# A list schedule with smaller margins in the first batch of an attention and mixture-of-experts kernel

## The chip, the core and the metric

The kernel runs on one core of a Trainium2 chip. The metric is the device time of one execution, in microseconds. The kernel before took 1354.56 us, the median of three runs of 1352.25, 1354.79 and 1354.56 us.

The core has a tensor engine (PE, with PEld for the loading of its stationary operand), a vector engine (DVE), a scalar engine (ACT), GpSimd (POOL) and a queue engine (SP) that issues most of the transfers. Each engine works through its own list of instructions in order; an instruction waits for those of other engines on which it depends.

## The reference

```python
# q, k, v: [8 batches, 8 heads, 576 positions, 64]; tau = 0.02
scores = scale * np.matmul(q, k.transpose(0, 1, 3, 2))
thresh = np.max(scores, axis=-1, keepdims=True) - tau
scores = np.where(scores >= thresh, scores, -1e9)
attn = np.exp(scores - np.max(scores, axis=-1, keepdims=True))
attn = attn / (np.sum(attn, axis=-1, keepdims=True) + 1e-09)
attn_out = np.matmul(attn, v)
# x: the heads of a position side by side, [4608 tokens, 512]
gate = 1.0 / (1.0 + np.exp(-(x @ w_gate)))        # w_gate, w_val: [512, 1536]
return (gate * (x @ w_val) @ w_out)               # w_out: [1536, 512]
```

A softmax whose scores more than tau under the row's maximum are left out, a product with V, and then a gated layer over all tokens. All numbers are fp32.

## The kernel before, in words

**Tiles.** Attention is done in 32 visits, one for each batch and pair of heads. A visit has nine tiles of 128 rows by 576 keys: for each of its two heads a group "00" and "02" (first head), "10" and "12" (second head) of two tiles each, and one leftover tile "l" with the last 64 rows of both heads. For one tile, PE makes the scores into one of two buffers `s` (L591 in batch 0, from plain fp32 operands; L599 from batch 1 on, from operands split in a high and a low part), DVE takes the row maximum (L606), the threshold is made from it (L615, on POOL for the first 36 tiles and on DVE from then on), ACT takes the exponential (L620), and DVE masks and sums in one pass (L623), the last to read `s`. For a group, DVE makes the reciprocals of the sums (L655), POOL scales both tiles (L657), PE transposes them (`tp`, L668; `lk`, L681), ACT copies the transposed tiles out of PSUM (`pt`, `pl`, L630), and after the second head PE multiplies with V (`av`, L704), once for tiles 0 and 1, once for tiles 2, 3 and l. ACT copies this to `xf`, and ACT and POOL split it in a high and a low part, the `x` of the gated layer (L714, L716).

**The gated layer.** Blocks 0, 1 and 2 are batches 0 to 2; a block has 24 units of a product with the gate's or value's weights (`m`, L764) and then its output units (`o`, L807). Batches 3 to 8 (the ninth being the leftover rows) go in pairs (L1006, L1071), with sums of blocks and seven products in place of eight. Batches 0 and 1 hand their x over in SBUF, batch 2 through memory (`xa`), the later ones through memory in another layout; `AWAY` is the first batch that goes through memory.

**Weights.** 36 pieces of weights are converted while attention runs (the helper `convert`): a load, a bit step on POOL (L424), an absolute value on ACT (L428), two bit steps on DVE (L431, L437), the high part on ACT (L449), the low part on POOL (L455; for pieces 18 to 23 on DVE, L451), and a store to memory. Twelve stay in SBUF for block 0. `CONV_IN` gives the due time of piece j of the gate's and value's weights, (first, step).

**What sets the order.** A list scheduler (`Plan`) gets all these operations with an engine, a modelled cost, a key (due time, in tiles) and the buffers that they need. It runs through modelled time: an engine that is free takes, among the operations that are ready and have their buffers, that with the lowest key. An operation is ready when what it depends on is done; if that is on another engine, a margin `LAG` is added for its own engine. The order that comes out is emitted, and nothing is moved after that. A tile's operations have the tile's number as key; the product with V that of the visit's last tile, less 0.7. PE's operations of the gated layer have keys above all of attention, so PE takes one only when none of attention is ready; the layer's other operations go first. `SHIFT` is added to the tile numbers from batch 1 on. `LK` gives the small copy of `lk` to ACT below tile 300 and to DVE above. `AHEAD_TWO` is how many units ahead the weights of the paired blocks are loaded.

Of the kernel before, what the change touches and what calls it, by code (L numbers as in the profile page):

```python
# [43 lines left out]
class Plan:  # L44
# [74 lines left out]
    def run(self):  # L119
        engines = ("PE", "DVE", "ACT", "POOL", "SP")  # L120
        ready = {e: [] for e in engines}
        free = {e: True for e in engines}
        events, now, n, dma = [], 0.0, 0, 0.0
        for o in self.ops:
            if not o.n_deps:
                heapq.heappush(events, (0.0, n, "ready", o))
                n += 1
        self.left = {}
        order = []
        while True:  # L130
            moved = True
            while moved:
                moved = False
                for e in engines:
# [3 lines left out]
                    while ready[e]:  # L138
                        x = heapq.heappop(ready[e])
# [30 lines left out]
            while events and events[0][0] <= now + 1e-9:  # L170
                _, _, kind, x = heapq.heappop(events)
                if kind == "free":
                    free[x] = True
                elif kind == "ready":
                    heapq.heappush(ready[x.eng], (x.key, x.seq, x))
                else:
                    for b in x.bufs:
                        b.users -= 1
                        if not b.users and b.held:
                            self.held[b.tag] -= 1  # L180
                            self.held[b.tag, b.cls] -= 1
                    for s in x.succ:
                        lag = 0.0 if s.eng == x.eng else LAG[s.eng]
                        s.ready = max(s.ready, now + lag + s.lag)
                        s.n_deps -= 1
                        if not s.n_deps:
                            n += 1
                            heapq.heappush(events, (s.ready, n, "ready", s))
# [13 lines left out]
    "w": 8, "t2": 6,  # L202
}
LEAD = 8
CONV_IN, CONV_OUT = (10, 1.5), (56, 3)


EARLY = 16
# [2 lines left out]
PAD = 64  # L211

NPS = 4

AV_COST = 0.0096

# [21 lines left out]

OWN = 12

SHIFT = 50


def LO_DVE(j, out):
# [4 lines left out]

LAG = {"PE": 1.2, "DVE": 0.3, "ACT": 0.08, "POOL": 0.3, "SP": 0.08}  # L250

WARM = 16

FIRST_PAIRS = 4
# [3 lines left out]

SUMS_IN, SUMS_OUT, SUM_KEY = {1: (0,), 2: (1,)}, {0: (0,), 1: (1,)}, 1000

AWAY = 2
AHEAD_TWO = 8

X_BY = ((("POOL",) * 4, ("DVE",)),) + ((("DVE",) * 4, ("DVE",)),) * 2
G_BY = (("POOL", "DVE", "POOL", "DVE"), ("DVE",))
# [19 lines left out]
def kernel(  # L285
# [25 lines left out]
    nc = tc.nc  # L311

    B, NPAIR, P, SK = k.shape
    D = v.shape[-1]
# [70 lines left out]
    op, buf = plan.op, plan.buf  # L385
# [9 lines left out]
    wo_d = {g: dram([P, ND, ND, 2, P], f"wod{g}") for g in range(NFG)}  # L395
    w_sb = {}

    def convert(i, f, key):

# [6 lines left out]
        raw = buf("w", [P, DM, 2], I32, f"wr{name}")  # L406
# [5 lines left out]
        def load():  # L412
# [7 lines left out]
        op("SP", 1.6, key - 6, load, writes=[raw], leave=3)  # L420
        lo, hi = (lambda: raw.ap[:, :, 0]), (lambda: raw.ap[:, :, 1])

        bt = buf("b", [P, DM], F32, f"wb{name}", "conv")
# [5 lines left out]
           reads=[raw], writes=[bt])  # L429
        a = lambda: bt.ap.bitcast(I32)  # L430
# [202 lines left out]
    class Group:  # L633
# [52 lines left out]
        def output(self, c, key):  # L686

            vis, pt, pl = self.vis, self.pt, self.pl
            last = self.tiles[0] != 0
            W = 2 * P + (SL if last else 0)  # L690
            av = buf("b", [P, W], F32, f"av{self.name}", "att")
# [6 lines left out]
                ms += [(2 * P, W, j, lambda h, j=j: c.pt.ap[:, 0, j, sl(h)]) for j in range(NJ)]  # L698
                ms += [(2 * P, W, NJ + 1, lambda h: c.pl.ap[:, 0, sl(h)])]

            def go():
                for i, (a, z, j, m) in enumerate(ms):
                    for h in range(2):
                        nc.tensor.matmul(  # L704
                            av.ap[h * D : (h + 1) * D, a:z], vis.vs.ap[:, j, h], m(h),
                            start=i == 0, stop=i == len(ms) - 1, skip_group_check=True,
                        )

            op("PE", AV_COST * W, key, go,
               reads=[pt, pl] + ([c.pt, c.pl] if last else []) + [vis.vs], writes=[av], also=[vis.xf])  # L710
            last_att[0] = copy(AV(vis.first), W, key, lambda: vis.xf.ap[:, c0 : c0 + W], av, (vis.xf, self.name))

    def split_x(x, c0, c1, xf, key):
# [425 lines left out]

    def conversions():  # L1140
        for j in range(2 * NF):
            convert(j % 2, j // 2, CONV_IN[0] + CONV_IN[1] * j)
        for f in range(NF):
            convert(2, f, CONV_OUT[0] + CONV_OUT[1] * f)

    def attention(vis):
        vis.prepare(LEAD)
# [138 lines left out]
```

## Time and profile before

The profiled execution took 1353.87 us; its span on the core is 1352.1 us and its mean granted TensorE clock 0.992.

| engine | busy, us | share of the span | instructions |
|---|---|---|---|
| PE | 1320.8 | 98% | 8292 |
| PEld | 1084.1 | 80% | 8292 |
| DVE | 954.8 | 71% | 1943 |
| ACT | 726.9 | 54% | 1339 |
| POOL | 630.3 | 47% | 660 |

Transfers moved 317.83 MB. The rows below are read like this. In the windows, each stretch of the span has the busy time of each engine, and in brackets how many instructions began in it; then the granted clock of PE (1.00 is full speed), the share of the time in which the 16 DMA engines were busy, and GB/s. In the groups, an instruction's line, engine and operation stand with what it writes <- what it reads, its shapes and its count; then busy time and the mean duration of one in ns; then the idle time of the engine ahead of it, and what ended most of this. A row of the timeline has the start and the duration in us; in square brackets stands the engine's idle time ahead of it and what ended that. The first 109 us hold batch 0's attention, with the conversions; the first unit of the gated layer starts at 108.72 us, the first output unit of block 0 at 232.7 us.

### The profile page before, as it was taken

To read this page: it belongs to the slowest core of one execution; us is meant where nothing else is said; L and a number is where in the kernel's file an instruction comes from. 1 tells how busy PE (TensorE), PEld (TensorE's weight loads), DVE (VectorE), ACT (ScalarE), POOL (GpSimd) and SP (SyncE) were. 2 spreads that over 40 slices of the span, in tenths; PEclk is the share of its full clock that TensorE was granted. 3 is DMA by queue.
4 is the path that set the end of the run, shared out by engine and by line. 5 is a ranking of instruction groups with operands and counts; after the bars stand their busy time and mean duration, and the time that the engine had idled before them with its cause. 6 is when DMAs were issued, how large, how long until landed. Compare 5 with 4: busy or idle time off the path is not lost.

```text
span 1352.1 us, 23686 instructions
## 1 busy us (share of the span) xinstructions
PE 1320.8 (98%) x8292; PEld 1084.1 (80%) x8292; DVE 954.8 (71%) x1943; ACT 726.9 (54%) x1339; POOL 630.3 (47%) x660
## 2 busy tenths in 40 slices
PE   7879999999999999999999999999999999999998
PEld 4557888888888888888888878888888888888887
DVE  7889868567877777778787763556965569654594
ACT  7878766666766766667776653223532225322242
POOL 6985957956777764967776741101000110001100
PEclk8989999999999999999999999999999999999999
DMA  9879999897978988898897858656695656756564
GB/s 341 279 251 309 311 257 269 233 279 209 264 212 242 261 242 227 250 267 238 238 270 188 241 179 295 205 180 211 201 308 183 201 193 204 249 180 204 186 221 129
DMA packets 140436, 317.83 MB, mean 235 GB/s; under 512 B 22048, under 2 KB 49952, under 8 KB 140320
## 3 DMA queue, kind: packets, MB, share of 16 engines
q1 hardware_dynamic: 140176, 316.33, 76.5%
q8 instruction: 67, 1.10, 0.4%
q14 instruction: 49, 0.40, 0.1%
q10 hardware_dynamic: 144, 0.00, 0.0%
HBM read 210.37 MB, written 54.53 MB: 196 GB/s over the span
## 4 chain that ended last, share of the span: by engine, by line
PE 87%; DMA 6%; DVE 2%; ACT 2%; issue 1%; POOL 1%; SPq 1%; ACTq 0%; DVEq 0%; POOLq 0%
PE m L764 13%; PE qb L1006 11%; PE av L704 11%; PE s L599 8%; PE qc L1006 7%; PE qa L1006 7%; PE tp L668 7%; PE o L807 6%; PE rb L1071 5%; PE rc L1071 4%; PE ra L1071 4%; DMA wo<-wod 2%; DMA kd<-k 2%; PE s_l L599 1%; PE lk L681 1%
## 5 line engine op out<-in xcount | busy, mean ns | idle before, releaser
L657 POOL TENSOR_SCALAR p<-p,zero_t,sm 128x576 f32<-128x576 f32 x256 | 216.3, 856 | 107.9 <-DVE sm L655 76.5
L606 DVE TENSOR_REDUCE st<-s 128x1 f32<-128x576 f32 x256 | 192.3, 754 | 91.9 <-PE s L599 83.2
L623 DVE SCALAR_TENSOR_TENSOR p<-s,st,p 128x576 f32<-128x576 f32 x256 | 205.9, 812 | 30.2 <-ACT p L620 23.9
L620 ACT ACTIVATE p<-s,st 128x576 f32<-128x576 f32 x256 | 190.2, 750 | 57.4 <-DVE st L606 56.5
L919 POOL TENSOR_TENSOR gA<-gA 128x512 f32<-128x512 f32 x18 | 24.1, 1341 | 416.2 <-DVE gA L985 416.2
L630 ACT COPY pt<-tp 128x512 f32<-128x512 f32 x256 | 147.4, 589 | 54.0 <-PE tp L668 51.9
L599 PE MATMUL s<-kd,qd 128*128 128x288 f32 x896 | 165.0, 308 | 3.7 <-issue 1.6
L668 PE MATMUL tp<-ident,p 128*128 128x128 f32 x1024 | 156.7, 282 | 2.5 <-POOL p L657 2.0
L764 PE MATMUL m<-x,wi 128*128 128x512 f32 x576 | 158.9, 403 | 0.0
L668 PEld LDWEIGHTS tp<-ident,p 128*128 128x128 f32 x1024 | 123.2, 143 | 29.4 <-POOL p L657 7.6
L599 PEld LDWEIGHTS s<-kd,qd 128*128 128x128 f32 x896 | 133.9, 190 | 14.6 <-DVE p_l L623 2.4
L704 PE MATMUL av<-pt,vs 128*64 128x256 f32 x1024 | 126.1, 389 | 0.0
L807 PE MATMUL o<-g,wo 128*128 128x512 f32 x432 | 117.5, 401 | 0.0
L943 DVE TENSOR_TENSOR qu<-qb,qp 128x512 f32<-128x512 f32 x72 | 49.8, 692 | 89.9 <-PE qb L1006 77.1
L764 PEld LDWEIGHTS m<-x,wi 128*128 128x128 f32 x576 | 99.9, 189 | 14.3
L1006 PE MATMUL qa<-xs_p,wa 128*128 128x512 f32 x432 | 109.6, 389 | 0.0
L704 PEld LDWEIGHTS av<-pt,vs 128*64 128x64 f32 x1024 | 68.6, 138 | 48.5 <-issue 7.5
L1006 PEld LDWEIGHTS qa<-xs_p,wa 128*128 128x128 f32 x432 | 81.1, 188 | 16.8
L807 PEld LDWEIGHTS o<-g,wo 128*128 128x128 f32 x432 | 75.5, 189 | 10.9
L630 ACT COPY xf<-av 128x256 f32<-128x256 f32 x64 | 25.6, 399 | 77.4 <-PE av L704 73.1
L911 ACT CAST gs_p<-gA 128x512 fp32r<-128x512 f32 x54 | 32.4, 620 | 64.5 <-DVE gA L985 26.5
L981 ACT ACTIVATE gA<-qa 128x512 f32<-128x512 f32 x18 | 10.8, 598 | 103.4 <-PE qa L1006 103.4
(148 smaller groups left out, 2628.3 us busy)
## 6 DMA issues: line engine op xcount, KB each, us to landing
kd<-k SPq DMA_DIRECT2D x112, 320.0 KB, 6.0
wi<-wid SPq DMA_DIRECT2D x48, 512.0 KB, 6.9
wo<-wod SPq DMA_DIRECT2D x36, 512.0 KB, 7.0
wa<-wid SPq DMA_DIRECT2D x36, 512.0 KB, 4.1
ws<-sid SPq DMA_DIRECT2D x36, 512.0 KB, 4.5
wt<-sid SPq DMA_DIRECT2D x36, 512.0 KB, 3.3
wo_p<-sod SPq DMA_DIRECT2D x36, 512.0 KB, 4.6
qd<-q SPq DMA_DIRECT2D x112, 128.0 KB, 4.6
```

The costliest lines, as they stand in the source:

```text
L599: nc.tensor.matmul(s.ap[:, c, :HALF], st(), mv(slice(kc + c * HALF, kc + (c + 1) * HALF)), start=m == 0, stop=m == len(steps) - 1,)
L606: op("DVE", 0.76, key, lambda: nc.vector.tensor_reduce(out=st.ap[:, 0:1], in_=sv(), axis=AX.XY, op=ALU.max, negate=True), reads=[s], write ...
L620: op("ACT", 0.74, key, lambda: nc.scalar.activation(p(), sv(), AF.Exp, bias=st.ap[:, 0:1], scale=1.0), reads=[s, (st, 0)], writes=[(g.p, i)])
L623: op("DVE", 0.9, key, lambda: nc.vector.scalar_tensor_tensor(out=p(), in0=sv(), scalar=st.ap[:, 1:2], in1=p(), op0=ALU.is_ge, op1=ALU.mult ...
L630: return op("ACT", act(n), key, lambda: nc.scalar.copy(dst(), src.ap), reads=[src], writes=[part])
L657: op("POOL", 0.9, key, lambda i=i: nc.gpsimd.tensor_scalar(out=p.ap[:, i * S : (i + 1) * S], in0=p.ap[:, i * S : (i + 1) * S], scalar1=zer ...
L668: nc.tensor.matmul(tp.ap[:, c, :], self.p.ap[:, o + c * P : o + (c + 1) * P], ident, is_transpose=True, start=c == 0, stop=c == NJ - 1, sk ...
L704: nc.tensor.matmul(av.ap[h * D : (h + 1) * D, a:z], vis.vs.ap[:, j, h], m(h), start=i == 0, stop=i == len(ms) - 1, skip_group_check=True,)
L764: nc.tensor.matmul(m.ap, wv[:, a, c * P : (c + 1) * P], xs[c].ap[:, z, c0:c1], start=e == 0, stop=e == 11,)
L807: nc.tensor.matmul(acc.ap, wv[:, f, a], g[fg * ND + f].ap[:, z], start=(fg, f, a, z) == (0, 0, 0, 0), stop=(fg, f, a, z) == (NFG - 1, ND - ...
L1006: nc.tensor.matmul(acc.ap, wv[:, y, (2 * h + c) * P : (2 * h + c + 1) * P], xt[prod][c].get()[:, z], start=e == 0 and prod in FIRST, stop= ...
L1071: nc.tensor.matmul(acc.ap, w.ap[:, e, c, y], gt[prod][2 * g + c].get()[:, z], start=m == 0 and g == 0 and prod in FIRST, stop=m == 5 and g ...
```

## The change

Six edits of numbers and one of code:

- A margin of its own, `FRONT_LAG`, holds for an operation whose key is under 36, which is batch 0: 0.3 for PE in place of 1.2, 0.2 for DVE and POOL in place of 0.3. The others keep `LAG`.
- In batch 0 the product with V is handed to the scheduler in three parts of about equal count, with a key later by 1.5 and a modelled cost by columns.
- `CONV_IN` goes from (10, 1.5) to (12, 2.6): piece j is due 2 + 1.1 j tiles later.
- `SHIFT` goes from 50 to 15: batch 1's tiles and all later ones have numbers lower by 35. The last visits thereby fall under tile 300, and 20 small copies go from DVE to ACT.
- `AWAY` goes from 2 to 1: batch 1 too hands its x over through memory.
- `AHEAD_TWO` goes from 8 to 7.
- An operation that depends on none starts at its own `lag`; this is 0 for all, and so are `NOT_YET` and `OUT_NOT_YET`.

```diff
-                heapq.heappush(events, (0.0, n, "ready", o))
+                heapq.heappush(events, (o.lag, n, "ready", o))
...
-                        lag = 0.0 if s.eng == x.eng else LAG[s.eng]
+                        lag = 0.0 if s.eng == x.eng else (FRONT_LAG if s.key < FRONT else LAG)[s.eng]
...
-CONV_IN, CONV_OUT = (10, 1.5), (56, 3)
+CONV_IN, CONV_OUT = (12, 2.6), (56, 3)
...
+AV_PARTED, AV_PARTS, AV_LATE = 1, 3, 1.5
...
-SHIFT = 50
+SHIFT = 15
...
 LAG = {"PE": 1.2, "DVE": 0.3, "ACT": 0.08, "POOL": 0.3, "SP": 0.08}
 
+FRONT, FRONT_LAG = 36, {"PE": 0.3, "DVE": 0.2, "ACT": 0.08, "POOL": 0.2, "SP": 0.08}
+
+NOT_YET, OUT_NOT_YET = (0.0, 0.0), 0.0
...
-AWAY = 2
-AHEAD_TWO = 8
+AWAY = 1
+AHEAD_TWO = 7
...
-            def go():
-                for i, (a, z, j, m) in enumerate(ms):
-                    for h in range(2):
-                        nc.tensor.matmul(
-                            av.ap[h * D : (h + 1) * D, a:z], vis.vs.ap[:, j, h], m(h),
-                            start=i == 0, stop=i == len(ms) - 1, skip_group_check=True,
-                        )
-
-            op("PE", AV_COST * W, key, go,
-               reads=[pt, pl] + ([c.pt, c.pl] if last else []) + [vis.vs], writes=[av], also=[vis.xf])
+            n = AV_PARTS if vis.b < AV_PARTED else 1
+            step = -(-len(ms) // n)
+            for lo in range(0, len(ms), step):
+                def go(lo=lo):
+                    for i in range(lo, min(lo + step, len(ms))):
+                        a, z, j, m = ms[i]
+                        for h in range(2):
+                            nc.tensor.matmul(
+                                av.ap[h * D : (h + 1) * D, a:z], vis.vs.ap[:, j, h], m(h),
+                                start=i == 0, stop=i == len(ms) - 1, skip_group_check=True,
+                            )
+
+                cost = AV_COST * W if n == 1 else 0.2 + 0.0018 * sum(z - a for a, z, *_ in ms[lo : lo + step])
+                op("PE", cost, key + (AV_LATE if n > 1 else 0), go,
+                   reads=[pt, pl] + ([c.pt, c.pl] if last else []) + [vis.vs], writes=[av], also=[vis.xf])
```

Three places show how the order moves. In the names the first number behind the letter is the pair of heads, then the group, in it the tile, and last a running number; the lines of the changed kernel lie 6 to 12 higher from L591 on.

**First piece: PE at the end of batch 0**, from the last product with V (`av_3_12`) to the first unit of the gated layer (`m_0_0_0`); `s_0`, `tp_0` and `lk_0` are batch 1's already. Before:

```order
L704 MATMUL av_3_12_1362<-pt_3_02_1212,vs_3_559 64x256 x8
L704 MATMUL av_3_12_1362<-pl_3_02_1233,vs_3_559 64x128 x4
L704 MATMUL av_3_12_1362<-pt_3_l_1170,vs_3_559 64x64 x8
L704 MATMUL av_3_12_1362<-pl_3_l_1173,vs_3_559 64x64 x2
L668 MATMUL tp_0_000_1403<-ident,p_0_00_1289 128x128 x4
L668 MATMUL tp_0_001_1412<-ident,p_0_00_1289 128x128 x4
L681 MATMUL lk_0_00_1420<-ident,p_0_00_1289 128x128
L599 MATMUL s_0_021_1425<-kd_0_0_686,qd_0_0_950 128x288 x4
L764 MATMUL m_0_0_0_1457<-x_0_572,ws_0_320 128x512 x3
L764 MATMUL m_0_0_0_1457<-x_1_873,ws_0_320 128x512 x3
```

Now:

```order
L715 MATMUL av_3_12_1367<-pl_3_02_1237,vs_3_548 64x128 x4
L715 MATMUL av_3_12_1367<-pt_3_l_1173,vs_3_548 64x64 x8
L715 MATMUL av_3_12_1367<-pl_3_l_1177,vs_3_548 64x64 x2
L605 MATMUL s_0_020_1414<-kd_0_0_677,qd_0_0_955 128x288 x4
L605 MATMUL s_0_021_1424<-kd_0_0_677,qd_0_0_955 128x288 x4
L674 MATMUL tp_0_000_1434<-ident,p_0_00_1307 128x128 x4
L674 MATMUL tp_0_001_1445<-ident,p_0_00_1307 128x128 x4
L687 MATMUL lk_0_00_1455<-ident,p_0_00_1307 128x128
L674 MATMUL tp_0_l_1462<-ident,p_0_l_1379 128x128 x4
L687 MATMUL lk_0_l_1471<-ident,p_0_l_1379 128x128
L605 MATMUL s_0_100_1479<-kd_0_1_969,qd_0_1_1137 128x288 x4
L776 MATMUL m_0_0_0_1487<-x_0_557,ws_0_324 128x512 x3
```

The product still stands as one run. Ahead of the first unit there are now the transposes of `0_l` and the scores of tile `0_100`, which stood behind eight of the unit's matmuls.

**Second piece: ACT in the first visit**, from the exponential of tile `0_00` on. Before:

```order
L620 ACTIVATE p_0_00_215<-s_0_001_204,st_0_001_213 128x576
L558 ACTIVATE qp_1_186<-qp_1_186,scale_t 128x576 x2
L620 ACTIVATE p_0_l_245<-s_0_l_228,st_0_l_239 128x576
L620 ACTIVATE p_0_02_248<-s_0_020_235,st_0_020_243 128x576
L428 ACTIVATE wb_0_257<-wr_0_192 128x512
L630 COPY pt_0_00_263<-tp_0_000_251 128x4x128
L630 COPY pt_0_00_263<-tp_0_001_265 128x4x128
L630 COPY pl_0_00_280<-lk_0_00_271 128x128
L620 ACTIVATE p_0_02_248<-s_0_021_276,st_0_021_290 128x576
```

Now:

```order
L626 ACTIVATE p_0_00_215<-s_0_001_203,st_0_001_213 128x576
L626 ACTIVATE p_0_l_247<-s_0_l_230,st_0_l_242 128x576
L564 ACTIVATE qp_1_190<-qp_1_190,scale_t 128x576
L636 COPY pt_0_00_257<-tp_0_000_250 128x4x128
L636 COPY pt_0_00_257<-tp_0_001_259 128x4x128
L636 COPY pl_0_00_274<-lk_0_00_267 128x128
L564 ACTIVATE qp_1_190<-qp_1_190,scale_t 128x576
L626 ACTIVATE p_0_02_280<-s_0_020_238,st_0_020_245 128x576
L434 ACTIVATE wb_0_291<-wr_0_199 128x512
```

The exponential of tile `020` (the first of `p_0_02`) stood ahead of the copies of `pt_0_00`; now it stands behind them, the copy of `pl_0_00` and the second scaling of `qp_1`.

**Third piece: POOL at the end of batch 0**, from the thresholds of the last tiles to the low part of the last `x` (`x_3`). Before:

```order
L615 TENSOR_SCALAR st_3_121_1237<-st_3_121_1237,ntau_t 128x1
L424 TENSOR_SCALAR wa_0_1259<-wr_0_1210,zero_t 128x512
L455 TENSOR_TENSOR ws_1_1269<-wa_1_1103,ws_1_1269 128x512
L657 TENSOR_SCALAR p_3_12_1235<-p_3_12_1235,zero_t,sm_3_12_1243 128x576 x2
L424 TENSOR_SCALAR wa_1_1315<-wr_1_1219,zero_t 128x512
L657 TENSOR_SCALAR p_0_00_1289<-p_0_00_1289,zero_t,sm_0_00_1311 128x576 x2
L424 TENSOR_SCALAR wa_0_1387<-wr_0_1313,zero_t 128x512
L518 TENSOR_TENSOR k_1_1357<-kn_1_450,k_1_1357 128x640
L716 TENSOR_TENSOR x_3_1417<-xf_3_1325,x_3_1417 128x512
```

Now:

```order
L621 TENSOR_SCALAR st_3_121_1250<-st_3_121_1250,ntau_t 128x1
L430 TENSOR_SCALAR wa_1_1279<-wr_1_1229,zero_t 128x512
L663 TENSOR_SCALAR p_3_12_1252<-p_3_12_1252,zero_t,sm_3_12_1277 128x576 x2
L461 TENSOR_TENSOR ws_1_1291<-wa_1_1179,ws_1_1291 128x512
L430 TENSOR_SCALAR wa_2_1335<-wr_2_1267,zero_t 128x512
L524 TENSOR_TENSOR k_1_1359<-kn_1_516,k_1_1359 128x640
L430 TENSOR_SCALAR wa_0_1383<-wr_0_1319,zero_t 128x512
L663 TENSOR_SCALAR p_0_00_1307<-p_0_00_1307,zero_t,sm_0_00_1317 128x576 x2
L663 TENSOR_SCALAR p_0_l_1379<-p_0_l_1379,zero_t,sm_0_l_1409 128x576
L728 TENSOR_TENSOR x_3_1422<-xf_3_1333,x_3_1422 128x512
```

The low part of a weight (`ws_1`) stood ahead of the scaling of `p_3_12` and now stands behind it. The keys `k_1` stand ahead of the scaling of `p_0_00` in place of behind it, and the scaling of `p_0_l` stands ahead of `x_3`.

More of the change, by code (lines that the diff above doesn't have):

```diff
@@ L396, with convert @@
     w_sb = {}
-    def convert(i, f, key):
+    def convert(i, f, key, not_yet=0.0):
         name = f"{f}_{i}"
@@ L418, in load @@
                 )
-        op("SP", 1.6, key - 6, load, writes=[raw], leave=3)
+        op("SP", 1.6, key - 6, load, writes=[raw], leave=3, lag=not_yet)
         lo, hi = (lambda: raw.ap[:, :, 0]), (lambda: raw.ap[:, :, 1])
@@ L1141, in conversions @@
         for j in range(2 * NF):
-            convert(j % 2, j // 2, CONV_IN[0] + CONV_IN[1] * j)
+            convert(j % 2, j // 2, CONV_IN[0] + CONV_IN[1] * j, max(0.0, NOT_YET[0] + NOT_YET[1] * j))
         for f in range(NF):
-            convert(2, f, CONV_OUT[0] + CONV_OUT[1] * f)
+            convert(2, f, CONV_OUT[0] + CONV_OUT[1] * f, OUT_NOT_YET)
     def attention(vis):
```

## The prediction

> **What bounds the kernel now.** I read the page first, then the span cut into windows.
>
> ```profile
> span 1352.1 us, 23686 instructions
> PE 1320.8 (98%) x8292; PEld 1084.1 (80%) x8292; DVE 954.8 (71%) x1943; ACT 726.9 (54%) x1339; POOL 630.3 (47%) x660
> ```
>
> ```profile
> core 0: us, PE busy (x) PEld busy (x) DVE busy (x) ACT busy (x) POOL busy (x), PEclk, DMA share, GB/s
> 0.00:10.00 10.00, 6.48 (x34) 4.88 (x34) 3.41 (x10) 4.63 (x7) 1.24 (x8) 1.00 0.79 254
> 10.00:20.00 10.00, 7.91 (x43) 4.96 (x43) 8.96 (x20) 9.06 (x17) 8.31 (x13) 0.83 1.03 411
> 20.00:30.00 10.00, 7.33 (x34) 4.30 (x34) 9.83 (x18) 8.14 (x16) 10.00 (x14) 0.69 1.02 373
> 30.00:40.00 10.00, 9.84 (x98) 6.24 (x94) 8.68 (x18) 8.72 (x17) 8.93 (x13) 0.97 0.88 303
> 40.00:50.00 10.00, 6.98 (x36) 4.41 (x37) 8.50 (x19) 7.90 (x16) 9.59 (x15) 0.83 0.74 256
> 50.00:60.00 10.00, 7.41 (x64) 4.70 (x64) 9.42 (x21) 7.85 (x16) 7.79 (x12) 1.00 0.93 285
> 60.00:70.00 10.00, 8.52 (x79) 5.28 (x75) 8.90 (x20) 8.19 (x17) 9.30 (x13) 1.00 0.87 297
> 70.00:80.00 10.00, 8.80 (x74) 5.48 (x76) 9.87 (x21) 8.36 (x16) 9.29 (x14) 1.00 0.90 248
> 80.00:90.00 10.00, 7.42 (x69) 4.77 (x66) 8.31 (x18) 7.41 (x15) 8.82 (x13) 0.93 0.94 292
> 90.00:100.00 10.00, 7.50 (x41) 5.93 (x41) 7.68 (x18) 7.37 (x15) 7.44 (x11) 0.73 0.44 176
> 100.00:110.00 10.00, 9.68 (x96) 7.76 (x93) 9.82 (x22) 8.63 (x19) 7.79 (x8) 1.00 0.79 265
> 110.00:230.00 120.00, 118.06 (x786) 97.96 (x785) 97.25 (x215) 85.25 (x160) 81.30 (x80) 1.00 0.97 292
> 230.00:300.00 70.00, 70.00 (x543) 58.49 (x542) 45.81 (x115) 44.81 (x86) 53.69 (x56) 1.00 0.93 250
> 300.00:700.00 400.00, 398.64 (x3101) 334.21 (x3100) 304.56 (x721) 274.89 (x521) 279.55 (x288) 1.00 0.85 242
> 700.00:817.00 117.00, 115.46 (x882) 95.50 (x880) 81.20 (x207) 70.59 (x124) 73.06 (x74) 1.00 0.73 214
> 817.00:1347.00 530.00, 530.00 (x2343) 438.98 (x2339) 331.93 (x494) 165.10 (x284) 54.23 (x40) 1.00 0.64 211
> ```
>
> From 817 to 1347 us PE is busy all of 530.00. Over 110 to 817 it idles 1.94 + 0 + 1.36 + 1.54 = 4.8 us. In the first 110 us its column adds up to 87.9: 22.1 us idle. PE's work is the same in both kernels, and behind 110 us there is always some of it ready, so the end moves by what the idle time of the first 110 us moves, and by any new idle time later. DVE is the fullest engine there: from 10 to 110 us its column is 90.0, so 10.0 us of it are free. The waits of PE up to 105 us say what it mostly stood for (total, times, longest):
>
> ```profile
> PE s L591 <- DVE p L623: 13.0, 12, 2.4
> ```
>
> Scores have two buffers; one comes free when the masking pass (L623) on DVE has read it. PE waits for DVE, DVE for PE and ACT: a ring.
>
> **The change part by part.** Shares of DVE up to 104 us, by groups:
>
> ```profile
> L623 DVE SCALAR_TENSOR_TENSOR p<-s,st,p 128x576 f32<-128x576 f32 x34 | 27.3, 814 | 4.9 <-ACT p L620 2.3 <-POOL st L615 2.0 <-POOL ws L455 0.4
> L606 DVE TENSOR_REDUCE st<-s 128x1 f32<-128x576 f32 x34 | 25.0, 752 | 5.5 <-PE s L591 4.7 <-PE s L599 0.7
> L431 DVE SCALAR_TENSOR_TENSOR wb<-wb,wa 128x512 int32<-128x512 int32 x19 | 13.1, 689 | 0.4 <-ACT wb L428 0.2
> ```
>
> *Less work in the front? No.* The new due times for weights (12 + 2.6j) look as if conversions left the first batch. By the order they don't: before the last mask of batch 0, DVE has 36 reductions, 36 masks and 18 pairs of conversion steps before, 19 after. A pair is two steps of one shape, 2 x 0.69 = 1.4 us more. So nothing but DVE's 10.0 us can be gained, the 19th pair coming off the stretch behind.
>
> *The three parts of the product: 0.* All eight products of batch 0 stand as one run of 12 or 22 matmuls in the new order too (the first piece of order above shows the last): no score got between the parts. Parting removes no instruction; the late key (+1.5) is spent by the smaller margin, and the products stand one tile of scores earlier. If a part did wait for an own signal, it would cost a few tenths each; I take 0.
>
> *First visit: a loss.* ACT at the start of before:
>
> ```profile
> 12.06 0.73 ACT L620 ACTIVATE p<-s,st 128x576 f32<-128x576 f32 x1
> 13.24 1.07 ACT L630 COPY pt<-tp 128x512 f32<-128x512 f32 x2
> 14.19 0.29 ACT L630 COPY pl<-lk 128x128 f32<-128x128 f32 x1
> ```
>
> ```profile
> 11.07 1.97 PE L668 MATMUL tp<-ident,p 128*128 128x128 f32 x8
> ```
>
> Now the exponential that began at 12.06 stands behind two copies, a small copy and a second scaling (second piece of order). The copies need the transposes, which end at 11.07 + 1.97 = 13.04. So 13.04 + 0.54 (second copy, half of 1.07) + 0.29 + 0.7 (the scaling, of the exponential's shape, by its 0.73) gives 14.6: 2.5 us late. Its mask, the score buffer behind the mask and the next conversion step are queued behind it. Going on by hand through the new order with these durations, I find the ninth tile 2.5 us late.
>
> *Visits 2 to 4: regained.* One of DVE's longest waits further on in before:
>
> ```profile
> 86.49 0.82 DVE L623 SCALAR_TENSOR_TENSOR p<-s,st,p 128x576 f32<-128x576 f32 x1 [1.00 <-ACT p L620]
> ```
>
> In the new order one or two conversion steps (0.69 each) stand between the reductions and the masks at such places, so DVE has work while ACT makes the exponential. By hand the lag falls to about 1.2 us at tile 27 and 0.7 at the last mask of batch 0, with the 19th pair done: 0.7 us ahead in work.
>
> *The tail of batch 0: a gain.* Rows of before:
>
> ```profile
> 96.05 0.81 DVE L623 SCALAR_TENSOR_TENSOR p<-s,st,p 128x576 f32<-128x576 f32 x1
> 97.78 1.28 POOL L455 TENSOR_TENSOR ws<-wa,ws 128x512 fp32r<-128x512 f32 x1 [2.07 <-DVE st L606]
> 99.04 1.65 POOL L657 TENSOR_SCALAR p<-p,zero_t,sm 128x576 f32<-128x576 f32 x2
> 106.94 0.80 DVE L623 SCALAR_TENSOR_TENSOR p_l<-s_l,st_l,p_l 128x576 f32<-128x576 f32 x1
> 107.80 1.27 POOL L716 TENSOR_TENSOR x<-xf,x 128x512 fp32r<-128x512 f32 x1
> 108.72 2.11 PE L764 MATMUL m<-x,ws 128*128 128x512 f32 x8
> 112.33 0.77 PE L599 MATMUL s<-kd,qd 128*128 128x288 f32 x4
> ```
>
> The last mask ends at 96.86, but its scaling on POOL starts at 99.04, behind a conversion (97.78) that was itself waiting. In the new order that conversion stands behind the scaling (third piece of order): with the mask at 97.5, scaling starts at 97.7, 1.3 us sooner. But POOL now has the scaling of the leftover tile ahead of x's low part, and that waits for its mask, which by hand through DVE's order ends at 106.4 (107.7 in before). The scaling (0.8) ends at 107.4, and x's low part at 107.4 + 1.27 = 108.7, against 109.07: of the 1.3 us, 0.4 are left for x. The score of tile 100 needs the mask of tile 020, by hand at 108.6, so that the first m starts at about 109.7. PE meanwhile does tp_l, lk_l and one more score, which in before came behind the first eight m. Eight m, these and that score are done at 112.33 + 0.77 = 113.1 in before, and by hand at 109.7 + 2.11 = 111.8 now: **1.3 us sooner**.
>
> *The rest: 0, with room.* Batch 1's x now goes through memory too, 4 stores and 4 loads like these:
>
> ```profile
> xa<-xa SPq DMA_DIRECT2D x4, 256.0 KB, 6.7
> ```
>
> 2.1 MB at 292 GB/s is 7 us of transfers where the DMA share is already 0.97; block 1's first unit comes only 30 tiles after block 0's first output unit, which covers it; uncovered, one landing, 6.7 us, would show. The earlier batch 1 (SHIFT) puts more tiles between the units of block 0: 49 tiles over its 24 input units for 37 before; PE has work in either mix. AHEAD_TWO 7 still loads several units ahead, where PE is busy 530.00 of 530. The zero allowances move nothing. Twenty small copies go from DVE to ACT in the last batch, both far from full there.
>
> **Sum.** 1353.87 (the profiled execution, 1.77 over its span; the median shown, 1354.56, is 0.7 above it) - 1.3 = **1352.6 us**. Bounds: if nothing of the first visit's 2.5 us comes back and the tail gives 1.3, +1.2, so 1355.1; if all of DVE's 10.0 us goes, 1343.9.
>
> **Rivals.**
>
> *A, the ring closes.* Window 70 to 80 has DVE at 9.87 of 10 with pairs of scores, the pattern that the new order has from tile 20 on. If 10 us free become 3, less 1.4 for the 19th pair: -5.6, so 1348.3. Against it: the first visit starts late, and half of the front is like 70 to 80 already. Chance 0.24.
>
> *B, the clock.* The granted clock is 0.83, 0.69, 0.97, 0.83, 0.93 and 0.73 in six of the windows; busy time by the missing share is 1.3 + 2.3 + 0.3 + 1.2 + 0.5 + 2.0 = 7.6 us of PE. If the long waits vanish, half of it goes with them: 1352.6 - 3.8 = 1348.8. Against: DVE, not PE, is the fullest. Chance 0.14. The Trainium skill (TensorE: Matmul & The Clock Gate, part 1) has the clock halved only after an idle window of about 3.4 us. Here the longest single wait was 2.4 us and the clock fell all the same, so the trace doesn't bear that limit out; by it this rival would be worth nothing.
>
> *C, slower: the wait moves behind the front.* Groups from 110 to 230 us of before:
>
> ```profile
> L599 PE MATMUL s<-kd,qd 128*128 128x288 f32 x128 | 23.2, 304 | 0.8 <-DVE p L623 0.6 <-DVE p_l L623 0.2
> L668 PE MATMUL tp<-ident,p 128*128 128x128 f32 x120 | 18.1, 275 | 0.0
> L704 PE MATMUL av<-pt,vs 128*64 128x256 f32 x96 | 11.7, 385 | 0.0
> L615 DVE TENSOR_SCALAR st<-st,ntau_t 128x1 f32<-128x1 f32 x33 | 6.9, 210 | 0.6
> ```
>
> A tile costs PE 23.2/32 + 18.1/30 + 11.7/32 = 1.7 us and DVE 0.81 + 0.75 + 0.21 = 1.8. Twelve more tiles between the units of block 0 make the window of 120 us 140 long and DVE's 97.25 some 118.5: from 81% to 84.5%. At 81% PE idled 1.6% (1.94 of 120); at 90%, from 10 to 110 us, 18.6%. On the line between, 84.5% costs 8.2% of 140 us: 11.5, and 9.5 more than now. The margins there are unchanged, so I take two thirds: 1352.6 + 6.3 = 1358.9. It decides once PE idles over 4 us between block 0's first input and first output unit. Chance 0.16.
>
> **Numbers.** The forecast has 0.46, mostly 1350 to 1357. A change under 0.2% (2.7 us about the median: 1351.9 to 1357.3) can't be told from none. A and B, with the forecast's lower edge (0.03): faster 0.41. C with the upper edge: slower 0.15. The rest, 0.44: same. The range, 1346.5 to 1358.5, leaves out half of A's lower side and the upper half of C.
>
> **What would show it.** Right: first m at 109 to 110 us with a tp_l and one score more ahead of it; a mask about 2 us later near 13 us; PE's wait for DVE masks still 10 us or more; products in single runs. Wrong: first m before 106 (A), PEclk near 1.00 in all windows to 110 (B), or more than 4 us of PE idle between 110 and 260 (C).

## The result: slower, and the profile after

The changed kernel took 1362.97 us, the median of four runs from 1361.77 to 1364.24. The kernel before, with one run more beside it, has 1354.67 us. The ratio is 1.0055, with an interval of 1.0033 to 1.0078. The forecast was 1352.6 with a range of 1346.5 to 1358.5: wrong in sign, and outside the range. The time of rival C (1358.9) is the nearest.

The page of the profile of the changed kernel, an execution of 1364.24 us:

```profile
span 1362.5 us, 23701 instructions
PE 1325.5 (97%) x8292; PEld 1085.2 (80%) x8292; DVE 954.0 (70%) x1923; ACT 733.6 (54%) x1359; POOL 626.9 (46%) x660
```

PE does the same 8292 matmuls. The span is 10.4 us longer: PE's busy time is 4.7 us longer and its idle time 5.7. Part of the former is the clock: by its record PE had 27.3 us at half clock ahead of 1340 us, in place of 20.5, which is worth up to 3.4 us; the rest of it was not traced. The windows of the changed kernel say where; of the columns, the busy times of PE, PEld, DVE, ACT and POOL come first:

```profile
0.00:110.00 110.00, 86.19 (x630) 56.44 (x630) 90.33 (x186) 86.88 (x161) 87.61 (x125) 0.89 0.85 289
110.00:230.00 120.00, 115.50 (x816) 94.35 (x816) 100.08 (x216) 83.98 (x159) 72.86 (x74) 1.00 0.92 276
230.00:300.00 70.00, 70.00 (x524) 59.34 (x519) 52.70 (x128) 49.18 (x93) 57.51 (x59) 1.00 0.87 267
300.00:700.00 400.00, 395.31 (x3003) 329.42 (x3001) 290.28 (x689) 264.57 (x503) 274.34 (x283) 1.00 0.83 243
700.00:817.00 117.00, 117.00 (x893) 98.54 (x892) 86.61 (x208) 79.33 (x152) 77.25 (x80) 1.00 0.72 212
817.00:1347.00 530.00, 530.00 (x2390) 437.88 (x2389) 331.91 (x498) 169.71 (x294) 57.31 (x43) 1.00 0.64 213
```

Up to 110 us PE idles 23.8 us, against 22.1 before. From 110 to 817 it idles 4.5 + 0 + 4.7 + 0 = 9.2 us, against 4.8. The larger part of the new idle time, 4.4 of 5.7 us, stands where the prediction had put nothing. PE's waits in the changed kernel (total, times, longest), up to 112 us and then from 112 to 830:

```profile
PE s L597 <- DVE p L629: 7.9, 11, 2.1
PE tp L674 <- POOL p L663: 4.4, 6, 1.1
PE tp_l L674 <- POOL p_l L663: 2.5, 3, 1.3
```

```profile
PE tp L674 <- POOL p L663: 3.0, 3, 1.6
PE s L605 <- DVE p_l L629: 1.3, 1, 1.3
PE tp_l L674 <- ACT xf L636: 1.3, 1, 1.3
```

In batch 0, 5 us of waiting for the mask are gone, and waiting for POOL's scaling came in their place (6.9 us, 1.8 before). Behind it, PE stops for single waits of 1 to 1.6 us. One of them, from POOL's and PE's timelines of the changed kernel:

```profile
409.23 1.29 POOL L800 TENSOR_TENSOR g<-th,g 128x512 fp32r<-128x512 f32 x1
415.01 1.28 POOL L870 TENSOR_TENSOR s<-wi 128x512 f32<-128x512 f32 x1 [4.48 <-DMA wi<-wid]
416.26 1.63 POOL L663 TENSOR_SCALAR p<-p,zero_t,sm 128x576 f32<-128x576 f32 x2
...
417.15 0.66 PE L674 MATMUL tp<-ident,p 128*128 128x128 f32 x4 [1.64 <-POOL p L663]
```

POOL stands 4.48 us at `s`, a sum of two parts of a weight that the paired blocks need only hundreds of microseconds later. The weight has not landed. The scaling of `p`, which attention needs now, stands behind it in POOL's list, and PE waits for that. The plan lets a sum start only behind its load, but it has loads land sooner than they do: the scheduler gives a load of 512 KB 1.5 us to start, 1.7 on one common channel and 0.9 to land, while the page of before has 6.9 us from issue to landing for `wi`.

### The profile page after: what moved, and what is told of

It is laid out like the page before. It is cut to its first block, busy times and chain, and to the rows that moved or that the text cites. A ratio compares the mean times of both kernels' runs of the same rounds, so it can differ in the third digit from the quotient of the medians.

```text
span 1362.5 us, 23701 instructions
## 1 busy us (share of the span) xinstructions
PE 1325.5 (97%) x8292; PEld 1085.2 (80%) x8292; DVE 954.0 (70%) x1923; ACT 733.6 (54%) x1359; POOL 626.9 (46%) x660
## 4 chain that ended last, share of the span: by engine, by line
PE 84%; DMA 4%; POOL 3%; DVE 3%; issue 2%; ACT 2%; SPq 1%; POOLq 0%; ACTq 0%; DVEq 0%
PE m L776 12%; PE qb L1018 11%; PE av L715 9%; PE s L605 7%; PE qc L1018 7%; PE qa L1018 7%; PE tp L674 7%; PE o L819 6%; PE rb L1083 5%; PE rc L1083 4%; PE ra L1083 4%; DMA wr<-in_moe_w_out_dram 2%; PE s_l L605 1%; POOL p L663 1%; PE lk L687 1%
## 5 line engine op out<-in xcount | busy, mean ns | idle before, releaser
L612 DVE TENSOR_REDUCE st<-s 128x1 f32<-128x576 f32 x256 | 192.8, 754 | 93.3 <-PE s L605 83.8
L931 POOL TENSOR_TENSOR gA<-gA 128x512 f32<-128x512 f32 x18 | 24.1, 1340 | 409.3 <-DVE gA L997 409.3
```

Source lines behind the costliest of these rows:

```text
L612: op("DVE", 0.76, key, lambda: nc.vector.tensor_reduce(out=st.ap[:, 0:1], in_=sv(), axis=AX.XY, op=ALU.max, negate=True), reads=[s], write ...
```

## Experiments

Ratios are to the kernel before, run on the same chip beside each group. "Sums waiting" is how long POOL stood for a load ahead of a sum `s<-wi`, from 112 to 830 us. The first sum of any weight starts at 227 us or later in every trace.

### Which part of the change

The change without its part behind batch 0 (margins and the three parts stay):

```diff
-CONV_IN, CONV_OUT = (12, 2.6), (56, 3)
+CONV_IN, CONV_OUT = (10, 1.5), (56, 3)
-SHIFT = 15
+SHIFT = 50
-AWAY = 1
-AHEAD_TWO = 7
+AWAY = 2
+AHEAD_TWO = 8
```

> Only the margins below key 36 and the three parts are changed; due times of weights, SHIFT, AWAY and AHEAD_TWO as before. Theory F (the loss is made in batch 0 and by the margins alone): about 1363 us, as the changed kernel. Theory M (two losses: some 4 us in the first 115 us from the margins, and some 6 us behind it, because batch 1 goes through memory and its attention runs ahead of the gated layer): first unit 3 to 4 us later than 108.7 and PE idle from 110 to 230 us as before (about 2 us), so 1358 to 1359. Theory O (each edit only reshuffles the order, and single stalls decide): anything from 1353 to 1363, with the loss at another place.

Measured: 1.0070 (1.0048 to 1.0091). The other way round, with the margins and the product of before:

```diff
-AV_PARTED, AV_PARTS, AV_LATE = 1, 3, 1.5
+AV_PARTED, AV_PARTS, AV_LATE = 0, 3, 1.5
-FRONT, FRONT_LAG = 36, {"PE": 0.3, "DVE": 0.2, "ACT": 0.08, "POOL": 0.2, "SP": 0.08}
+FRONT, FRONT_LAG = -9, {"PE": 0.3, "DVE": 0.2, "ACT": 0.08, "POOL": 0.2, "SP": 0.08}
```

> Margins and product with V as before; CONV_IN, SHIFT, AWAY and AHEAD_TWO as in the change. Theory F: about 1354.7, as before. Theory M: the first 110 us cost at most 1 us more than before, PE idles 4 us or more between 110 and 230, and the time is 1359 to 1360. Theory O: no fixed place; 1353 to 1363.

Measured: 1.0067 (1.0044 to 1.0091). Either half alone costs as much as the whole; both medians (1365.94 and 1366.55 us) lie above the 1363 that theory O allowed, beside 1356.64 for before. Then the memory path: taken out of the change, and put alone into the kernel before.

```diff
-AWAY = 1
+AWAY = 2
```

> The changed kernel, but batch 1 hands its x over in SBUF again (AWAY 2). In the order the units of block 0 then end at tile 79 in place of 91 (78 in the kernel before). Theory F: no change, 1363. Theory M: the 6 us behind the front go away and the 4 us of the front stay: 1357 to 1358, with PE idle from 110 to 230 near 2 us. Theory O: 1353 to 1363.

> The kernel before, with batch 1 handed over through memory (AWAY 1) and nothing else. In the order the first 190 rows of PE are those of before; block 0's first output unit stands at tile 83 in place of 78. Theory F: 1354.7. Theory M: front as before to 0.3 us, and part of the 6 us behind it, since fewer tiles come in between than with SHIFT 15: 1356 to 1359. Theory O: 1353 to 1363.

Measured: 1.0052 (1.0033 to 1.0071) without it, and 1.0037 (1.0019 to 1.0056) for it alone. In the fourth run the first 190 rows of PE are those of before, the first unit starts at 108.7 us as before, and the time is lost all the same. The last part, the smaller margins without the three parts and without the rest:

> The kernel before with the smaller margins alone (product with V in one part). Theory M: the front loses 3 to 4 us up to 115 us, as in the run with margins and parts together (2.4). Parts as the cause: the front is as before to 1 us. Behind the front, Theory O: 4 us or more are lost in addition, 1360 to 1366; Theory M: nothing more, 1358.

Measured: 1.0042 (1.0024 to 1.0061), the first unit at 116.5 us, and 35.9 us of sums waiting. No part has a price of its own that adds to the others. Theories F and M fall: F since the rear alone loses, M since taking a part out gives nothing back.

### Edits without purpose

If every edit loses, the edit may not matter. Two, and later a third, that change a number of the kernel before by 1 to 3%:

```diff
-LAG = {"PE": 1.2, "DVE": 0.3, "ACT": 0.08, "POOL": 0.3, "SP": 0.08}
+LAG = {"PE": 1.22, "DVE": 0.3, "ACT": 0.08, "POOL": 0.3, "SP": 0.08}
```

> The kernel before with PE's margin 1.22 in place of 1.2: an edit with no purpose. The order of PE differs from row 39 on. Theory O (the order of before is an uncommonly good draw; an edit of any kind gives a new draw, which is usually worse by 4 to 10 us through waits of over 1 us behind the front): 1357 to 1365, and PE idle from 110 to 830 us of 6 us or more in place of 4.9. Theory M (margins and memory each have their own price): 1353 to 1357, as before.

```diff
-AV_COST = 0.0096
+AV_COST = 0.0097
```

> The kernel before with the modelled cost of the product with V at 0.0097 a column in place of 0.0096: also without purpose. Theory O: 1357 to 1365, with waits at other places than in the run with the margin 1.22. Theory M: 1353 to 1357.

```diff
-LAG = {"PE": 1.2, "DVE": 0.3, "ACT": 0.08, "POOL": 0.3, "SP": 0.08}
+LAG = {"PE": 1.2, "DVE": 0.3, "ACT": 0.08, "POOL": 0.31, "SP": 0.08}
```

> The kernel before with POOL's margin 0.31 in place of 0.3: a third edit without purpose. Theory O: 1357 to 1365, and sums waiting for loads over 18 us. Theory M (before is no special draw): 1353 to 1357.

Measured: 1.0050 (1.0033 to 1.0067), 1.0016 (0.9999 to 1.0034), 1.0059 (1.0036 to 1.0082). Two of the three lose as much as the change. The order of before is a better draw than these neighbours, and the reading that fits all these runs is that the change is slower because it left this order; the second of the three edits can't be told from before. In the run with POOL's margin 0.31 a wait for a load reaches PE most plainly, with the weights of the output units (POOL and PE, timelines of that run):

```profile
591.86 1.26 POOL L858 TENSOR_TENSOR s_o<-wo 128x512 f32<-128x512 f32 x1 [7.01 <-DMA wo<-wod]
593.11 1.63 POOL L657 TENSOR_SCALAR p<-p,zero_t,sm 128x576 f32<-128x576 f32 x2
...
593.99 0.48 PE L668 MATMUL tp<-ident,p 128*128 128x128 f32 x1 [3.65 <-POOL p L657]
```

A sum stands 7.01 us for its load, the scaling stands behind it, and PE is idle for 3.65 us.

### More margin for PE

The other reading was that PE's margin of 1.2 us is too small for a plan that is off by several. Doubled behind batch 0, in the kernel before:

```diff
-LAG = {"PE": 1.2, "DVE": 0.3, "ACT": 0.08, "POOL": 0.3, "SP": 0.08}
+LAG = {"PE": 2.4, "DVE": 0.3, "ACT": 0.08, "POOL": 0.3, "SP": 0.08}
...
+FRONT, FRONT_LAG = 36, {"PE": 1.2, "DVE": 0.3, "ACT": 0.08, "POOL": 0.3, "SP": 0.08}
```

> The kernel before with PE's margin doubled to 2.4 from batch 1 on; batch 0 keeps 1.2 and its first 130 rows on PE. Theory W (behind the front PE stops where the plan is off by more than its margin): the waits between 130 and 700 us fall below 2 us, no clock window at half there, 1353 to 1356 unless the filler runs out at the end of attention (16 matmuls of output units are left behind it in place of 72). Theory O: just another draw, 1357 to 1365.

Measured: 1.0026 (1.0007 to 1.0046). The trace was of an execution with a span of 1352.4 us, and PE's idle time from 110 to 830 us was only 2.0. A second trace was taken without any edit, and one each of the kernel before and of the change:

> The order with PE's margin 2.4 behind the front once more. Its first trace had a span of 1352.4 us, with 2.0 us of PE idle from 110 to 830 us and 2.7 us behind, while its timed runs had a median of 1360. Theory C: the second trace is nearer to 1358 in span, with more windows at half clock in the first 115 us. Theory W alone: 1353 again.

> The kernel before once more, for a second trace of one and the same order. Theory C (executions of one order differ because the clock is granted in fixed windows of 3.4 us, whose phase against the kernel is chance): the order of waits is the same, but other windows up to 115 us are at half clock, and the span differs from 1352.1 by what these windows hold of PE, up to 4 us. If the waits themselves differ (transfers), idle time of PE moves by as much instead.

> The changed kernel once more, timed in the same way as the experiments. 1.004 to 1.008 of before. Theory O and C: the first 115 us again 2 to 4 us behind before, the waits behind the front at mostly the same places (near 165 and 575 us), and other windows at half clock.

Measured: the wide margin's second span is 1362.7 us, with 9.1 us idle from 110 to 830. So the low first value was one execution and not the order, and theory W, which gave 1353 to 1356, falls: the timed runs have a median of 1359.97. The change in its second timing has 1.0038 (1.0020 to 1.0057), its span there 1357.8. And the kernel before, the same order instruction by instruction, now shows:

```profile
span 1360.0 us, 23686 instructions
```

That is 7.9 us more than the trace from which the prediction was made. Single runs of the kernel before in the five groups of experiments lie between 1350.4 and 1364.97 us, with medians from 1355.2 to 1357.4. Of these 135 runs 20 were under the first trace's 1353.87 us, and 5 over the second's 1361.84: a low one and a high one of the same kernel. In the second trace ACT stood for a load, and PE behind it:

```profile
624.61 0.72 ACT L514 CAST k<-kn 128x640 fp32r<-128x640 f32 x1 [4.39 <-DMA kd<-k]
...
627.49 0.73 PE L764 MATMUL m<-x,wi 128*128 128x512 f32 x2 [1.28 <-ACT xf L630]
```

Theory C (only the phase of the clock's windows makes the difference) is not enough: PE had 20.5 us at half clock in both traces of before, and in that stretch the waits themselves moved, and by a load.

### The sums later

The test of theory D, that POOL stands at sums whose weights have not landed: the two first sums of a weight become ready in the plan 4 us later than their load's modelled landing, and nothing else is edited. First in the kernel before, then in the change:

```diff
-        def add(cost, out, x, y, sign, reads, writes):
+        def add(cost, out, x, y, sign, reads, writes, lag=0.0):
...
-            ), reads=reads, writes=writes)
+            ), reads=reads, writes=writes, lag=lag)
...
-            add(1.3, lambda t=t: full(t, 0), lambda x=x: full(x, 0), lambda x=x: full(x, 1), 1, [x], [t])
+            add(1.3, lambda t=t: full(t, 0), lambda x=x: full(x, 0), lambda x=x: full(x, 1), 1, [x], [t], 4.0)
```

> The kernel before, with 4 us of margin for the sums of weights on POOL behind the load that they read (0.3 before). The order is the same up to row 367 of PE. Theory D (behind the front POOL stands at a sum whose weights have not landed, 12.3 us in all in the trace of before, with the scaling of p queued behind it, and PE waits for that): POOL's waits of sums for loads fall under 5 us from 112 to 830 us, PE's waits for POOL there go to under 0.5 us, and the time is 1352 to 1356, not slower than before. Theory O (just another draw): 1357 to 1364.

> The changed kernel with the same 4 us of margin for the sums. Its traces have 19.8 and 27.4 us of POOL's sums waiting for loads and 2 to 4 us of PE waiting for POOL behind the front. Theory D: these go under 8 and under 0.5 us, and 3 to 4 us of the 6 come back, 1357 to 1359. Theory O: 1357 to 1366, whatever the waits.

Measured: 0.9989 (0.9968 to 1.0011) and 0.9978 (0.9963 to 0.9994). The change with this one margin is no longer slower than the kernel before; its median is 1355.57 us, beside 1357.42, and lower than the 1357 to 1359 that theory D gave it. POOL's waits for these loads, in before, in the change (first trace) and in the change with the margin:

```profile
POOL s L858 <- DMA wi<-wid: 12.3, 7, 5.2
```

```profile
POOL s L870 <- DMA wi<-wid: 19.8, 10, 5.5
```

```profile
POOL s L870 <- DMA wi<-wid: 4.6, 2, 2.7
```

The windows of the change with the margin:

```profile
0.00:110.00 110.00, 86.00 (x630) 56.10 (x630) 90.36 (x187) 86.76 (x161) 87.92 (x126) 0.89 0.85 289
110.00:230.00 120.00, 117.87 (x836) 97.48 (x837) 100.58 (x223) 86.15 (x164) 75.87 (x76) 1.00 0.93 285
230.00:817.00 587.00, 584.06 (x4476) 489.05 (x4475) 427.50 (x1021) 397.43 (x751) 412.49 (x419) 1.00 0.83 240
```

Up to 110 us nothing has changed against the change (86.00 for 86.19, the front's loss is still there). From 110 to 230 idle time is 2.1 us in place of 4.5, but PE's order is the same in both up to 261 us and the first sum comes at 249 us, so this is a difference between executions (the change's second trace has 3.6) and not the margin's. From 230 to 817 us, where the sums are, idle time is 2.9 us in place of 4.7 (3.0 in the second). From 112 to 830 PE waits 0.3 us for POOL's scaling in place of 3.0 (0.8 in the second). The span of this trace is 1354.3 us, 8.2 below that of the change's first.

Whether this holds for other orders: the edit without purpose that cost most, and the change without its front, both with the same 4 us.

> The edit without purpose that cost most (POOL's margin 0.31, ratio 1.0059), now with 4 us of margin for the sums of weights. Theory D: the loss goes, 0.997 to 1.002 of before. Theory O: 1.002 to 1.008 as for the other orders.

> Due times, SHIFT, AWAY and AHEAD_TWO of the change with the margins and the product with V of before (1.0067 without it), and 4 us of margin for the sums. Theory D: 0.996 to 1.001. Against the change with the same margin (0.9978) it shows what the smaller margins of batch 0 are worth: if they cost the 2 to 3 us that masks come late at the end of batch 0, this is at 0.996; if they gain, above 0.999.

Measured: 1.0007 (0.9987 to 1.0027), from 1.0059; and 0.9982 (0.9963 to 1.0000), from 1.0067. The table puts the pairs side by side.

| order | as it was | sums 4 us later | sums waiting, us | then | PE idle 230 to 817, us | then |
|---|---|---|---|---|---|---|
| before | 1 | 0.9989 | 12.3 and 3.9 | 0.3 | 2.9 and 5.9 | 2.7 |
| change | 1.0055, 1.0038 | 0.9978 | 19.8 and 27.4 | 4.6 | 4.7 and 3.0 | 2.9 |
| change behind batch 0 alone | 1.0067 | 0.9982 | 25.2 | 0.6 | 10.5 | 3.1 |
| POOL's margin 0.31 | 1.0059 | 1.0007 | 16.6 | 2.7 | 7.3 | 0.9 |

In all three slower orders the loss goes, and in the order of before, which has the shortest such waits, little is gained. The windows of the third pair show where, without the margin and with it:

```profile
230.00:817.00 587.00, 576.52 (x4376) 481.46 (x4376) 424.43 (x1016) 389.01 (x740) 408.64 (x417) 0.99 0.84 238
```

```profile
230.00:817.00 587.00, 583.86 (x4473) 489.06 (x4472) 424.32 (x1020) 394.23 (x751) 409.43 (x419) 1.00 0.84 241
```

That pair also prices the smaller margins together with the three parts: with the sums later the change has 0.9978 with them and 0.9982 without, no difference.

So the three runs show that the planned time of the sums carries the loss. How all of it reaches PE is not shown: PE's waits for the scaling are a part of its idle time (3.0 of 9.2 us in the change's first trace, 0.8 of 6.7 in the second), and the change without the memory path, slower by 0.52%, has none of them beside 18.4 us of sums waiting. Nor does the length of the sums' waits give the time of an execution: the slower trace of before has the shorter ones (3.9 us). A later sum also holds its weight's buffer longer, which can move later loads; no run separates this from the wait itself.

Last, 3 us for the operations of ACT, DVE and POOL with keys outside 1 to 35 that read what SP loads (the sums keep 4 in all):

```diff
+                        if x.eng == "SP" and s.eng in ("ACT", "DVE", "POOL") and not 1 <= s.key < FRONT:
+                            lag += LOAD_LAG
...
+LOAD_LAG = 3.0
```

> The change with 3 us of margin for every operation of ACT, DVE and POOL behind batch 0 that reads what SP loads (4 us for the sums): also x that comes from memory, and weights to be converted. If these waits cost as the sums do: 0.994 to 0.997 of before. If only the sums matter: 0.997 to 0.999, as the change with the margin for the sums.

Measured: 0.9981 (0.9964 to 0.9998), as the sums alone. The keys under 1 take in the first operations of batch 0, and the last mask there ends 2.0 us later than in the change (101.56 for 99.55). So the run shows no gain from the other loads, and doesn't price them by themselves.

### The clock in batch 0

```diff
+            for c in range(4):
+                nc.tensor.matmul(
+                    s.ap[:, c % 2, HALF : HALF + P], ident, ident, is_transpose=True, start=True, stop=True,
+                    skip_group_check=True,
+                )
```

> The order of before, with four small transposes into unused columns behind each plain score of batch 0 (about 0.4 us each time, 36 times; PE idles 22 us there). They keep PE busier in each clock window. Theory C: no window at half clock up to 105 us in place of six; PE's 7.6 us of lost clock come back as far as scores are waited for, so 1349 to 1353. If the dummies delay the real work instead: 1356 to 1362, at full clock all the same.

Measured: 1.0078 (1.0055 to 1.0101). The window of that run from 10 to 110 us:

```profile
10.00:110.00 100.00, 82.61 (x657) 55.78 (x658) 78.94 (x165) 72.65 (x140) 77.91 (x109) 0.97 0.79 263
```

The clock is at 0.97, against 0.90 before, and DVE does less: 78.9 us for 90.0. The last mask of batch 0 ends 12 us later, and the median, 1366.14 us, is above both forecasts. The dummies stand in the ring of scores and masks, which fits that they lengthen it by more than the clock gives back; so this run says what dummies cost there and not what a full clock is worth.

## Why the prediction was wrong, step by step

**What bounds the kernel: right, but too much read from one trace.** PE with filler behind 110 us, and the ring of scores and masks ahead of it, hold in all traces. But the sum was made against one execution, which was a low one of its kernel: 1353.87 us, where the groups have medians of 1355 to 1357. Behind 110 us its 4.8 us of idle time were taken as the property of any order. The second trace of the same order has 8.7 (2.8 + 0.2 + 5.7 + 0 in the same windows), and the edit without purpose that cost most has 15.7.

**The product in three parts, 0: right as to the order.** All products stand in single runs. No run took the parts out of the change alone. Without its part behind batch 0, the runs with the parts (1.0070) and without them (1.0042) have intervals that overlap.

**First visit, 2.5 us late: right in kind, over-sized.** The exponential began at 14.25 us (14.6 forecast), and the masks of visit 0 were 1.3 to 2.2 us late from the fourth on; the ninth was 1.5 late, for 2.5 forecast.

```profile
14.25 0.74 ACT L626 ACTIVATE p<-s,st 128x576 f32<-128x576 f32 x1
```

**Visits 2 to 4, lag down to 0.7 us: half right.** In the first trace the lag was gone by tile 16 and 1.3 us at tile 27 (1.2 forecast), but did not fall from there: at the last mask of batch 0 the change was 2.7 and 1.5 us late in its two traces. Five more traces with the order of before in batch 0 have this mask from 0.6 us earlier to 1.4 us later than the first one.

**The tail, a gain of 1.3 us: wrong.** The scaling of `p_3_12` did start sooner after its mask, at 99.94 for a mask that ended at 99.55. What the step missed is a new wait three instructions on, in POOL's timeline:

```profile
99.94 1.62 POOL L663 TENSOR_SCALAR p<-p,zero_t,sm 128x576 f32<-128x576 f32 x2 [0.94 <-DVE sm L661]
...
106.33 1.56 POOL L524 TENSOR_TENSOR k<-kn,k 128x640 fp32r<-128x640 f32 x1 [2.71 <-ACT k L520]
...
111.63 1.27 POOL L728 TENSOR_TENSOR x<-xf,x 128x512 fp32r<-128x512 f32 x1
```

The keys moved ahead of the next scaling, and POOL stood 2.71 us for their high part from ACT. x's low part began at 111.63 in place of 107.4, and the first unit at 114.26 in place of 109.7. The second trace has 112.75.

**The rest, 0 with room: the step that decided, wrong.** The part behind batch 0, priced at 0 here, costs 0.67% by itself (1.0067, some 9 us), and with the sums later nothing (0.9982). The step asked whether PE has work behind the front and whether transfers have time, and found both. It did not ask what stands at the head of each engine's queue: with POOL in order, a sum that waits for its load holds the scaling behind it, and work that PE has in plenty doesn't help, since PE's order is fixed too. The waits were there to be seen in the trace of before: 12.3 us in seven pieces, up to 5.2 us each, of which only 0.2 us reached PE as a wait for the scaling. Rival C's "The margins there are unchanged" was wrong as well: an operation of the gated layer on DVE or POOL has key -1, under 36, so `FRONT_LAG` holds not for batch 0 alone but for the layer's operations too. What this alone does was not run.

**Rival C** named the sign and about the time, and a place (110 to 260 us) that holds a part of the loss. Its test of more than 4 us of PE idle was met in the first trace (4.5 from 110 to 230), not in the second (3.6). DVE's share rose as it said, to 83.4% (100.08 of 120), but idle time doesn't follow this share: in the run of the change with the sums later it is 83.8% with 2.1 us of idle time, and in that of the part behind batch 0 with the sums later 81.4% with 6.1 us. There PE did wait for masks, as C has it (110 to 260 us of that run):

```profile
PE s L605 <- DVE p L629: 5.9, 3, 4.2
```

That run is nevertheless no slower than before (0.9982), so this wait isn't what decided. (The 0.15 for "slower" in the prediction's numbers is less than C's own 0.16, to which an edge of the forecast was to be added.) **Rivals A and B** need a front that gains; it lost in both traces. The doubt beside B stands: the clock falls without an idle window, and the last section gives the limit that the runs show.

What stays open: what the smaller margins cost. Masks do come late with them: in the four traces with the change's order in batch 0 (the two above, that without the memory path and that with the sums later) the last mask is 1.5 to 2.9 us behind the first trace of before, and with the order of before at most 1.4. But with the sums later the time is the same with these margins and without, so no price in time is shown. Nor is it shown what makes the idle time from 110 to 230 us, ahead of the sums.

## What to carry to other kernels

An order made by a planner has neighbours: before a change of its numbers is priced, time two or three edits without purpose, and compare with these and not with the one order that was kept. In an engine that works in order, look for operations that nobody needs soon and that read a load; give them the landing time that the profile shows, not the one the plan hopes for. One trace is one execution: here the same program gave spans of 1352.1 and 1360.0 us.

## What the runs showed of the hardware

**The clock needs no idle window.** The granted clock changes on a fixed grid of 3.41 us. Two groups of windows of the changed kernel, laid on this grid (the first to 0.05 us):

```profile
411.80:415.20 3.40, 3.40 (x21) 2.92 (x19) 3.03 (x9) 2.48 (x5) 0.19 (x1) 1.00 1.05 228
415.20:418.60 3.40, 1.76 (x13) 1.32 (x12) 2.01 (x7) 1.33 (x2) 3.39 (x4) 1.00 1.02 274
418.60:422.00 3.40, 3.40 (x27) 2.67 (x27) 2.72 (x5) 2.78 (x6) 3.33 (x5) 1.00 0.40 161
```

```profile
575.71:579.12 3.41, 3.41 (x39) 2.38 (x39) 3.41 (x1) 2.88 (x5) 3.41 (x4) 1.00 0.75 220
579.12:582.54 3.42, 1.95 (x25) 1.46 (x21) 3.38 (x7) 0.59 (x2) 2.88 (x4) 0.99 0.90 199
582.54:585.95 3.41, 3.41 (x12) 2.75 (x12) 3.07 (x9) 1.48 (x2) 3.41 (x4) 0.51 0.88 278
```

In the second group PE was busy for 1.95 us of the middle window's 3.42, with no wait over 1.35, and the next window ran at half clock: half of it, 1.7 us, is lost on top of the wait. In the first group it was busy for 1.76 of 3.40 and nothing followed. Counted over the 20 traces of this case up to 1340 us, of the windows at full clock with PE busy under 50%, 84 of 88 were followed by one at half; of those from 50 to 60%, 25 of 69; of those from 60 to 93%, none of 332. In one window that was followed by half clock, no wait was longer than 0.73 us. The Trainium skill (TensorE: Matmul & The Clock Gate, part 1) has such a free-running window of 3413 ns, which the grid agrees with, and lets the clock fall after an idle window; here a half-busy one is enough.

**One DVE instruction, 0.9 to 5.5 us.** The split of q in DVE's timeline of the change, while POOL was busy for all of 572.3 to 579.1 us:

```profile
574.93 5.48 DVE L527 SCALAR_TENSOR_TENSOR q<-qn,scale_t,q 128x640 fp32r<-128x640 f32 x1
```

The twenty-seven others of the same shape and line have a median of 1.3 us; in before the median is 0.9, and one takes 3.95. The masks, whose scores come from PSUM, show no such spread (0.80 to 0.83 us). PE's wait of 1.35 us that ends at 581.2, with the window at half clock after it, is behind this one. The Trainium skill (GPSIMD Engine Reference, section 1, Specifications) has DVE instructions with two SBUF inputs contend with GpSimd. The trace agrees: the split reads two such inputs, a mask one of them and one in PSUM. No run here took POOL's work away from beside the split.
